# Wave 0's second product by half blocks, an earlier weight queue, and one cast on another engine

## The chip, the cores and the metric

One NeuronCore of a Trainium2 chip. It has a matrix engine (TensorE, "PE" in the profile, with "PEld" for its weight loads), a vector engine (VectorE, "DVE"), a scalar engine (ScalarE, "ACT"), a general one (GpSimd, "POOL"), and a queue engine that issues most transfers (SyncE, "SP"). Each runs its own list of instructions in order and waits on semaphores for the others. The metric is the device time of one execution, in microseconds; less is better.

## The reference

Lightning attention over blocks of 64, its result laid out as tokens by features, then a feed-forward layer with a sigmoid gate:

```python
for b in range(nb):                     # blocks of 64 along the sequence, kv_state carried on
    intra = np.einsum('bhic,bhjc->bhij', qb, kb) * Dmask[None]
    intra = np.einsum('bhij,bhjd->bhid', intra, vb)
    inter = np.einsum('bhid,bhde->bhie', qb * lam_pow[None], kv_state)
    out[:, :, sl] = intra + inter
    kv_state = lam_block * kv_state + np.einsum('bhsd,bhse->bhde', kb * rev_pow[None], vb)
...
x = attn_out.transpose(0, 2, 1, 3).reshape(B * S, H * D)      # 3072 tokens x 512
h = x @ w_in                                                  # w_in 512 x 2048
g = h * (1.0 / (1.0 + np.exp(-1.702 * h)))
return g @ w_out                                              # w_out 2048 x 512
```

q, k and v are 4 batches x 8 heads x 768 x 64, float32.

## The kernel before

The 3072 tokens are worked in six waves of 512. Waves 0 and 1 (`ND = 2`) take two batches one after the other (`c` = 0 and 1, 256 tokens of each); waves 2 to 5 take 128 tokens of all four batches. A wave loads k, q and v; casts k and q to bf16 with the decay factors (`do_cast`); transposes them (`turn_pe` on TensorE in waves 0 and 1, `turn_dma` by transfer later); forms masked scores, state and output (`start` and `end` in waves 0 and 1); writes the attention result, transposed, to `xT`; then runs the feed-forward layer.

**First product** (`x @ w_in`, to 16 slices `fc` of `g_sb`). Wave 0 does it plainly: `mlp1_half` for slices 0 to 3 by batch, `mlp1` for 4 to 15. Wave 1 does half of its slices plainly (`mlp1_half`, the four pairs in `HALVES`, for both batches), and the rest, like waves 2 to 5, by a scheme of seven half-block products instead of eight (`in_product`, steps `a1`, `a7v`, ... in `STEPS`). That scheme needs sums of weight blocks (`in_sums(g)`, four VectorE operations or eight smaller ones for each of four groups `g`) and of `xT` blocks (`x_sums`, four operations).

**Second product** (`g @ w_out`). Wave 0 does it plainly in `mlp2(w, g, j)`: for each group `g` of 128 tokens and chunk `j` of w_out, four matmuls of 128x512, 64 in all; a VectorE copy of each finished group, and its two stores later. Waves 1 to 5 use the seven-product scheme: `product(w, n, ts)` runs product `n` for token tile `t` as eight matmuls of 128x256 into one of three accumulator banks (Q for n = 2; V for 7 and 4; X for 1, 6, 5, 3). Products 2, 4, 5, 3 complete an output block, and 1, 7, 6 leave a part that ScalarE copies out before the next product adds to the same bank (`after_product`). It needs sums of `g_sb` (`g_sums`, steps `gl..` for the low half of the slices, `gh..` for the high half; s1 to s4 of the step's digits) and of w_out chunks (`weight_sums(j)`, four operations for each of four chunks).

**Order.** Inside `manual_schedule` the order of the program is the order on each engine. `side` holds (position, function) pairs for attention and sums, `main` the matrix work of waves 0 and 1; a side item comes ahead of the main item of its number. Waves 2 to 5, and wave 1 from step `a1` on, follow the strings in `STEPS` by `one_step`. So the attention of wave 1 is threaded between the `mlp2` items of wave 0 (positions 19 to 34), `in_sums` stand at 5, 6, 7 and 10, `weight_sums(0..2)` at 14, and `weight_sums(3)` at 2.5 of wave 1's slices.

**Queues.** GpSimd issues the weight transfers, which convert to bf16 (w_in in five chunks of 2, 3, 4, 4 and 3 slices, w_out in four), and batch 1's v of wave 0, in between its own casts. SyncE issues k, q and v, the stores, and the DMA transposes, in program order. Wave 1's loads are kept behind a tiny transfer that reads w_out chunk 1 (`gate_sync`, line 710), so that they start when that chunk has landed. k and q have one buffer per batch slot, so a load waits for the cast of the data before it.

Of the kernel before, what the change touches and what calls it, by code (L numbers as in the profile page):

```python
# [25 lines left out]
def kernel(  # L26
# [13 lines left out]
    nc = tc.nc  # L40
# [3 lines left out]
    P = 128  # L44
# [398 lines left out]

    CHAIN = {1: "X", 6: "X", 5: "X", 3: "X", 2: "Q", 7: "V", 4: "V"}

    def product(w, n, ts):
        last = w == NW - 1
        key = ts[0] if last else 0
        if n == 1 and (last or ts[0] == 0):
            for c in "QVX":  # L450
                blocks[w, c, key] = acc(f"ps_{c}", shape=[P, 2, 256], tag="a" if last and ts[0] else "mm")
        bank = blocks[w, CHAIN[n], key]
        sums, raw = half_sum.get(w, [None] * 4), [[token_half(w, i, kh) for kh in range(2)] for i in range(2)]
        x = {1: raw[0][0], 2: raw[0][1], 4: raw[1][1], 5: sums[0], 6: sums[1], 7: sums[2], 3: sums[3]}[n]
        for t in ts:
            for m in range(FFC // 2):
                y = {1: (0, 0), 2: (1, 0), 3: (1, 1)}.get(n)
                y = w_half(m, *y) if y else TS[{4: 3, 5: 0, 6: 1, 7: 2}[n]][:, m]
                nc.tensor.matmul(bank[:, t], x[:, m, t * P : (t + 1) * P], y,  # L459
                                 start=(n in (1, 2, 7) and t == ts[0] * last and m == 0),  # L460
                                 stop=(m == FFC // 2 - 1), skip_group_check=True)
        if last or ts[-1] == 1:
            t = slice(ts[0], ts[0] + 1) if last else slice(0, 2)
            if n == 2 and 0 < w < NW - 1:
                c11[w] = partial(after_product, w, n, bank, t)
            else:
                after_product(w, n, bank, t)
# [27 lines left out]
    GR = {w: (1, 2, 0, 3) if w > 1 else (0, 3) for w in range(1, NW)}  # L495
    TAGS = {w: ("aQXV", "mXVQ", "aQXV", "aXVQ") if w > 1 else ("aQXV", "aXVQ") for w in range(1, NW)}
    HALVES = (0, 2, 5, 7)
    IN_SUMS_AT, X_AT, T_AT = ((5, 1), (6, 2), (7, 3), (10, 0)), 3.5, 2.5
    GROUPS = (((4, 13), (14, 15)), ((0, 2), (1, 3)), ((6, 5), (8, 7)), ((10, 9), (12, 11)))
    USED = sorted({g for w in range(NW) for g in GR.get(w, ())})  # L500
    TI = {g: [const.tile([P, KC // 2, 2, P], bf16, name=f"w_in_t{g}{n}") for n in range(1, 5)] for g in USED}
# [59 lines left out]
        a, b = (GROUPS[g][u][j] for u in range(2))  # L561
        nc.scalar.activation(g_of[w][:, a : b + 1 : b - a, 256 * i : 256 * i + 256], bank, GELU)  # L562

    late = []

    def mlp2(w, g, j):
        if j == 0:
            o_ps[w, g] = acc("ps_out", shape=[P, d_model], tag="mm")
        ps_out = o_ps[w, g]
        for fc in range(j * CW, (j + 1) * CW):  # L570
            nc.tensor.matmul(ps_out, g_of[w][:, fc, g * P : (g + 1) * P], w_out_sb[j][:, fc % CW, :],  # L571
                             start=(fc == 0), stop=(fc == FFC - 1))
        if j == NCH - 1:
            o = op.tile([P, d_model], f32, tag="o", name="o_sb")
            nc.vector.tensor_copy(o, ps_out)
            r0 = g // 2 * S + (g % 2) * P

            def store():
                for a, rows in enumerate((A, Z)):
                    nc.sync.dma_start(out=out[r0 : r0 + P].rearrange("(s a) d -> s a d", a=2)[:, a, :], in_=o[rows])  # L580
            late.append(store)

    def mlp_items(w):
        if w < ND:
            items = [(mlp1_half, w, c, fc) for c in range(HF) for fc in ((0, 2), HALVES)[w] if w or c or fc]
            if w == 0:
                items += [(mlp1, w, fc) for fc in range(4, FFC)]
        if w == 0:
            items += [(mlp2, w, g, j) for j in range(NCH) for g in range(3)]
            return items + [(mlp2, w, 3, j) for j in range(NCH)]  # L590
        return items + [(one_step, w, s) for s in STEPS[w].split()]

    def one_step(w, s):
        if s[0] == "+":
            w, s = w + 1, s[1:]
# [1 line left out]
        if s[0] == "f":  # L597
            mlp1(w, int(a))
        elif s[0] in "abcd":
            k = "abcd".index(s[0])  # L600
            in_product(w, GR[w][k], int(s[1]), TAGS[w][k], dve_copy if s[2:] == "v" else act_copy)
        elif s[0] in "ABCD":
            in_gelu(w, GR[w]["ABCD".index(s[0])], int(a))
        elif s[0] == "P":
            product(w, int(s[1]), (int(s[2]),))
        elif s[0] in "kq":
            do_cast(x, int(a), s[0], nc.vector)
        elif s[0] in "KQ":
            do_cast(x, int(a), s[0].lower(), nc.gpsimd)
        elif s[0] == "t":  # L610
            turn_dma(x, int(s[2]), s[1])
        elif s[0] == "v":
            cast_v(x, int(s[1]), ((act_copy, dve_copy)[s[2:] == "v"],))
        elif s[0] == "S":
            n_scores(x, int(a))
        elif s[0] == "M":
            n_masks(x, int(a))
        elif s[0] == "m":
            n_masks(x, int(a), True)
        elif s[0] == "R":  # L620
            n_rest(x)
        elif s[0] == "o":
            c11.pop(w)()
        elif s[0] == "X":
            x_sums(x)
        elif s[0] == "G":
            gate_pool(x_sum[w][3][0:1, 0, 0:1])
        elif s[0] == "g":
            m0, m1 = {"l": (0, 4), "h": (4, 8)}[s[1]]
            g_sums(w, m0, m1, tuple(int(c) - 1 for c in s[2:]))  # L630
        elif s[0] == "L":
            load(w + (1 if a == "w" else 2), "kq" if a == "k" else "v")
        else:
            raise ValueError(s)

    STEPS = {
# [24 lines left out]
    with tc.manual_schedule():  # L661
# [18 lines left out]
        d_scores(0, 0, 0)  # L680
        d_scores(0, 0, 1)
        fill(3)
        for g in range(2):
            do_cast(0, 1, "k", nc.gpsimd, g)
        for j in (1, 2):
            load_w_in(j)
        d_one(0, 0, "mm")
        d_keep(0, 0)
        turn_pe(0, 1, "k", act_copy, 0)
# [2 lines left out]
        d_state(0, 0, states[0, 0], Z)  # L692
        do_cast(0, 1, "q", nc.vector, 0)
        do_cast(0, 1, "q", nc.vector, 1)
        turn_pe(0, 1, "k", dve_copy, 1)
        d_x(0, 0, 0, oa, act_copy)
        turn_pe(0, 1, "q", act_copy, 0)
        d_inter(0, 0, oz, 0, False)
        turn_pe(0, 1, "q", dve_copy, 1)
        d_x(0, 0, 1, oz, act_copy)  # L700
        fill(1, "a")
        d_scores(0, 1, 0, True)
        cast_v(0, 1, (act_copy, pool_copy))
        for j in range(3, len(IN_CH)):
            load_w_in(j)
        for j in range(NCH):
            load_w_out(j)
        nc.gpsimd.affine_select(mask, mask, pattern=[[0, 1], [1, P]], channel_multiplier=-1, base=0,
                                compare_op=mybir.AluOpType.is_ge, fill=0.0)
        gate_sync(w_out_sb[1][0:1, 0, 0:2])  # L710
# [31 lines left out]
            if w and c == 0:  # L742
                d_keep(w, 1)

        def stores():
            for f in late:
                f()

        side, main = [(0, (end, 0, 1))], []
        for w in range(ND):  # L750
            n = len(main)
            main += mlp_items(w)
            e = len(main)
            x = w + 1
            if x < ND:
                for c, (k_at, q_at, v_at, k_turn, q_turn, s_at, e_at) in enumerate(
                        ((19, 20, 19, 24, 25.5, 27, 30), (26.5, 28, 28, 29, 30, 32, 34))):
                    side += [(n + k_at, (do_cast, x, c, "k", (nc.vector, nc.gpsimd)[c])),
                             (n + q_at, (do_cast, x, c, "q", nc.vector)),
                             (n + v_at, (cast_v, x, c, ((pool_copy, pool_copy), (act_copy, act_copy))[c])),  # L760
                             (n + k_turn, (turn_pe, x, c, "k", act_copy)),
                             (n + q_turn, (turn_pe, x, c, "q", act_copy)),
                             (n + s_at, (start, x, c)), (n + e_at, (end, x, c))]
            else:
                for c in range(HF):
                    for t, nm in ((n + (2.1, 4.1)[c], "k"), (n + (3, 5)[c], "q")):
                        side += [(t, (do_cast, x, c, nm, nc.gpsimd)), (t, (turn_dma, x, c, nm))]
                side += [(n + 1, (stores,)), (n + 7, (load, x, "v")), (n + X_AT, (x_sums, w)), (n + T_AT, (weight_sums, NCH - 1))]
            if w == 0:
                side += [(n + t, (in_sums, g)) for t, g in IN_SUMS_AT]  # L770
                side += [(n + 14, (weight_sums, j)) for j in range(NCH - 1)]
                side += [(n + 12, (load, w + 2, "kq"))]
        side.sort(key=lambda x: x[0])
        for i, (f, *a) in enumerate(main):
            while side and side[0][0] <= i:
                _, (g, *b) = side.pop(0)
                g(*b)
            f(*a)
        for _, (g, *b) in side:
            g(*b)  # L780
        for w in range(ND, NW):
            for s in STEPS[w].split():
                one_step(w, s)


# [28 lines left out]
```

## Time and profile before

| | |
|---|---|
| times of three runs | 193.36, 193.69, 196.18 us; median 193.69 |
| the profiled execution | 194.36 us, of it 192.7 us of span |
| granted TensorE clock | 1.00 in every stretch that was read |
| wave 1's first slice (line 414) | starts 49.89, the first complete in sequence at 50.05 |
| step a1 of wave 1 (line 543) | starts 58.83 |
| first scores of wave 2 (line 335) | start 67.27 |
| HBM | 27.26 MB read, 6.29 MB written |

The page gives busy time by engine, the span in 40 slices, the transfer queues, the chain of work that ended last, and the costliest groups of instructions. Other views of the same execution list the instructions in order of time, that chain in order of time, and busy time by stretch. Start times are counted from the start of the span. In the order of time, "x4" is the number of merged instructions, and the brackets at the end tell how long the engine had been idle and what ended that. Matmuls overlap, so a group's shown length is longer than the time until the next one can start.

### The profile page before, as it was taken

The page shows a single profiled execution, that of the slowest core. Times are in us where ns is not written, and L with a number is a line of the kernel's source. Part 1 is how long each engine was busy: PE and PEld are TensorE (multiplying, and loading weights), DVE is VectorE, ACT ScalarE, POOL GpSimd, SP SyncE. Part 2 cuts the span into 40 slices and gives each one's busy share as a digit, 9 for nine tenths or more (in the row PEclk, how much of TensorE's full clock was granted, in tenths as well). Part 3 has the DMA queues.
Part 4 walks back from the last instruction along what each step waited for, and adds up shares of the span by engine and source line. Part 5 has one row for each costly group of instructions (what it writes and reads, how often), then busy time and mean ns, then how long its engine had stood idle before and what let it go on. Part 6 is the DMA issues. An engine that isn't in the chain of part 4 may idle for free.

```text
span 192.7 us, 5432 instructions
## 1 busy us (share of the span) xinstructions
PE 184.8 (96%) x2243; PEld 146.3 (76%) x2249; DVE 152.2 (79%) x288; ACT 127.4 (66%) x238; POOL 50.9 (26%) x73
## 2 busy tenths in 40 slices
PE   7779999999999999999999999999999999999993
PEld 2357644446788888888888888888888888888882
DVE  1886775189799899878799979799879797889950
ACT  4867764035776886479896388896388885597711
POOL 5478200034593000097000195000393000000000
PEclk9999999999999999999999999999999999999999
DMA  5999999999989699874989846999366903300113
GB/s 160 315 239 196 198 200 207 262 274 282 242 222 194 127 258 240 212 180 113 209 202 223 247 113 156 210 231 250 136 141 139 218 0 110 113 0 3 48 58 111
DMA packets 89087, 33.90 MB, mean 176 GB/s; under 512 B 67431, under 2 KB 88423, under 8 KB 89063
## 3 DMA queue, kind: packets, MB, share of 16 engines
q1 hardware_dynamic: 84164, 28.84, 60.7%
q0 software_dynamic: 4896, 4.72, 14.5%
q8 instruction: 17, 0.28, 0.6%
q14 instruction: 8, 0.06, 0.1%
q10 hardware_dynamic: 2, 0.00, 0.0%
HBM read 27.26 MB, written 6.29 MB: 174 GB/s over the span
## 4 chain that ended last, share of the span: by engine, by line
PE 76%; DMA 16%; DVE 2%; POOL 2%; SPq 1%; issue 0%; ACT 0%; ACTq 0%
PE ps_X L459 18%; PE ps_hX L543 16%; PE ps_V L459 9%; PE ps_hV L543 8%; DMA w_out<-in_moe_w_out_dram 6%; PE ps_Q L459 5%; PE ps_hQ L543 4%; DMA kf<-in_k_dram 4%; DMA vf<-in_v_dram 3%; PE ps_out L571 3%; PE ps_h L414 3%; DMA qf<-in_q_dram 3%; PE ps_s L335 2%; PE ps_o L390 2%; POOL w_in L181 1%; PE ps_o L377 1%
## 5 line engine op out<-in xcount | busy, mean ns | idle before, releaser
L459 PEld LDWEIGHTS <-g_s 128*128 128x128 bf16 x320 | 30.9, 98 | 4.1
L562 ACT ACTIVATE g_sb<-h_sb 128x512 bf16<-128x512 f32 x54 | 32.6, 631 | 1.2 <-DVE h_sb L551 1.2
L543 PEld LDWEIGHTS <-w_in_t 128*128 128x128 bf16 x288 | 28.1, 98 | 3.8 <-issue 0.5
L221 ACT COPY part<-ps_hX 128x512 f32<-128x512 f32 x32 | 18.3, 586 | 11.9 <-PE ps_hX L543 11.9
L459 PEld LDWEIGHTS <-g_sb 128*128 128x128 bf16 x240 | 22.8, 98 | 3.4
L543 PEld LDWEIGHTS <-w_in 128*128 128x128 bf16 x216 | 21.1, 98 | 2.4
L543 PE MATMUL ps_hX<-x_s,w_in_t 128*128 128x256 bf16 x144 | 21.6, 272 | 0.0
L459 PE MATMUL ps_X<-w_out_t,g_s 128*128 128x256 bf16 x160 | 19.1, 273 | 0.0
L439 DVE TENSOR_TENSOR g_s<-g_sb 128x1024 bf16<-128x1024 bf16 x20 | 13.7, 687 | 5.8 <-ACT g_sb L562 5.6
L209 POOL TENSOR_TENSOR ks<-kf,k_pow 128x512 bf16<-128x512 f32 x16 | 16.6, 1062 | 3.1 <-PE ps_kv L279 3.1
L209 POOL TENSOR_TENSOR qs<-qf,q_pow 128x512 bf16<-128x512 f32 x16 | 16.6, 1062 | 2.0 <-PE ps_h L414 2.0
L656 POOL CAST behind_q<-x_s 1x1 f32<-1x1 bf16 x3 | 0.5, 175 | 62.3 <-DVE x_s L528 62.3
L218 DVE COPY part<-ps_hV 128x512 f32<-128x512 f32 x18 | 12.4, 688 | 3.2 <-PE ps_hV L543 3.2
L571 PE MATMUL ps_out<-w_out,g_sb 128*128 128x512 bf16 x60 | 14.3, 379 | 0.2
L551 DVE TENSOR_TENSOR h_sb<-part,ps_hX 128x512 f32<-128x512 f32 x18 | 12.3, 681 | 2.7 <-PE ps_hX L543 2.7
L551 DVE TENSOR_TENSOR h_sb<-part,ps_hV 128x512 f32<-128x512 f32 x18 | 12.3, 684 | 1.0 <-PE ps_hV L543 1.0
L221 ACT CAST v_sb<-vf 128x1024 bf16<-128x1024 f32 (+1 forms) x13 | 11.3, 884 | 2.2 <-DMA vf<-in_v_dram 2.2
L551 DVE TENSOR_TENSOR h_sb<-part,ps_hQ 128x512 f32<-128x512 f32 x18 | 12.2, 680 | 0.0
L562 ACT ACTIVATE g_sb<-ps_hX 128x512 bf16<-128x512 f32 x18 | 10.6, 588 | 1.8 <-PE ps_hX L543 1.8
L472 ACT COPY part<-ps_X 128x512 f32<-128x512 f32 (+1 forms) x12 | 6.1, 511 | 8.1 <-PE ps_X L459 8.1
L414 PE MATMUL ps_h<-xT,w_in 128*128 128x256 bf16 x96 | 11.3, 273 | 0.0
L348 DVE SCALAR_TENSOR_TENSOR sm<-ps_s,inv_pow,mask 128x512 bf16<-128x512 f32 x16 | 11.2, 744 | 0.0
(112 smaller groups left out, 362.4 us busy)
## 6 DMA issues: line engine op xcount, KB each, us to landing
kf<-in_k_dram SPq DMA_DIRECT2D x10, 512.0 KB, 7.0
qf<-in_q_dram SPq DMA_DIRECT2D x10, 512.0 KB, 6.6
vf<-in_v_dram SPq DMA_DIRECT2D x10, 512.0 KB, 6.1
out_dram<-o_sb SPq DMA_DIRECT2D x24, 128.0 KB, 2.4
out_dram<-o_sb SPq DMA_DIRECT2D x12, 256.0 KB, 2.1
w_out<-in_moe_w_out_dram POOLq DMA_DIRECT2D x4, 512.0 KB, 13.3
kf<-in_k_dram SPq DMA_DIRECT2D x4, 256.0 KB, 3.1
qf<-in_q_dram SPq DMA_DIRECT2D x4, 256.0 KB, 4.9
```

Source lines behind the costliest of these rows:

```text
L209: eng.tensor_tensor(x.rearrange("p b (r i j d) -> p j (b r) i d", i=2, j=2, d=D)[:, j], f.rearrange("p h (a d) -> p (h a) d", a=2).rearran ...
L218: nc.vector.tensor_copy(out, in_)
L221: nc.scalar.copy(out, in_)
L348: nc.vector.scalar_tensor_tensor(sm, s, inv_pow[:, n : n + 1], mask.to_broadcast([P, B, P]), op0=MUL, op1=MUL)
L414: nc.tensor.matmul(h[:, u, :], w_in_sb[j][:, kc, i * P : (i + 1) * P], xT[w][:, kc, cols], start=(kc == 0), stop=(kc == KC - 1))
L439: nc.vector.tensor_tensor(o, x, y, op=f)
L459: nc.tensor.matmul(bank[:, t], x[:, m, t * P : (t + 1) * P], y, start=(n in (1, 2, 7) and t == ts[0] * last and m == 0), stop=(m == FFC // ...
L472: nc.scalar.copy(part[w, n, t.start][:, t], bank[:, t])
L543: nc.tensor.matmul(bank[:, u], z[:, kc], y[:, kc], start=(n in (1, 2, 7) and u + kc == 0), stop=(kc == 1), skip_group_check=True)
L551: nc.vector.tensor_tensor(h, h_part[w, g, {2: 1, 5: 7, 4: 6}[n]], bank, op=ADD)
L562: nc.scalar.activation(g_of[w][:, a : b + 1 : b - a, 256 * i : 256 * i + 256], bank, GELU)
L571: nc.tensor.matmul(ps_out, g_of[w][:, fc, g * P : (g + 1) * P], w_out_sb[j][:, fc % CW, :], start=(fc == 0), stop=(fc == FFC - 1))
```

## The change

Wave 0 no longer has `mlp2`. Its second product is run by `product`, which gains an argument `ms`, the slice pairs to take: steps `p1a`, `p2a`, `p1b`, `p2b`, `p7l`, `p1h`, `p2h`, `p7h` run products 1, 2 and 7 in pieces by chunks of w_out, then `p4l`, `p4h`, and `P60` to `P31` as in other waves. `g_sums` for wave 0 and `weight_sums(3)` stand in wave 0. The positions of `side` and `main` give way to an order written out. `in_sums(2)` (step `I2`) moves to wave 1, behind `gh3`. Among GpSimd's instructions, w_in chunk 1 goes between the two halves of a k cast, and all other weight chunks directly behind it; half of wave 0's v cast of batch 1 goes from GpSimd to VectorE; wave 1's q cast of batch 1 goes from VectorE to GpSimd. Wave 0's stores are issued as its blocks are completed.

```diff
-    def product(w, n, ts):
+    def product(w, n, ts, ms=range(FFC // 2)):
...
-        if n == 1 and (last or ts[0] == 0):
+        if n == 1 and (last or ts[0] == 0) and ms[0] == 0:
...
-            for m in range(FFC // 2):
+            for m in ms:
...
-        if last or ts[-1] == 1:
+        if (last or ts[-1] == 1) and ms[-1] == FFC // 2 - 1:
             t = slice(ts[0], ts[0] + 1) if last else slice(0, 2)
-            if n == 2 and 0 < w < NW - 1:
+            if n == 2 and w < NW - 1:
...
+        elif s[0] == "p":
+            product(w, int(s[1]), (0, 1), {"a": range(4), "b": range(4, 6), "l": range(6), "h": range(6, 8)}[s[2]])
+        elif s[0] == "W":
+            weight_sums(int(a))
+        elif s[0] == "I":
+            in_sums(int(a))
...
-        1: ("a1 a7v a2 a6 b1 b7v A2 a5 b2 b6 B2 a4 a3 b5 b4 A5 P10 A4 b3 gl3 B4 B5 P11 gh3 S0 S1 M0 P20 m1 "
+        1: ("a1 a7v a2 a6 b1 b7v A2 a5 b2 b6 B2 a4 a3 b5 b4 A5 P10 A4 b3 gl3 B4 B5 P11 gh3 I2 S0 S1 M0 P20 m1 "
...
-        for g in range(2):
-            do_cast(0, 1, "k", nc.gpsimd, g)
-        for j in (1, 2):
+        do_cast(0, 1, "k", nc.gpsimd, 0)
+        load_w_in(1)
+        do_cast(0, 1, "k", nc.gpsimd, 1)
+        for j in range(2, len(IN_CH)):
             load_w_in(j)
+        for j in range(NCH):
+            load_w_out(j)
...
-        turn_pe(0, 1, "k", dve_copy, 1)
         d_x(0, 0, 0, oa, act_copy)
         turn_pe(0, 1, "q", act_copy, 0)
         d_inter(0, 0, oz, 0, False)
+        turn_pe(0, 1, "k", dve_copy, 1)
...
-        cast_v(0, 1, (act_copy, pool_copy))
-        for j in range(3, len(IN_CH)):
-            load_w_in(j)
-        for j in range(NCH):
-            load_w_out(j)
+        cast_v(0, 1, (act_copy, dve_copy))
...
+        end(0, 1)
+        for c, fc in ((0, 2), (1, 0), (1, 2)):
+            mlp1_half(0, c, fc)
+        for fc in range(4, FFC):
+            mlp1(0, fc)
+            steps(0, {5: "I1", 7: "I3", 9: "I0 gl3 gl1", 11: "W0 gl2", 13: "W1 gl4"}.get(fc, ""))
+        steps(0, "p1a gh3 p2a W2 p1b p2b p7l W3 p1h p2h p7h")
+        do_cast(1, 0, "k", nc.vector)
+        steps(0, "p4l")
+        do_cast(1, 0, "q", nc.vector)
+        turn_pe(1, 0, "k", act_copy)
+        steps(0, "p4h gh1 gh2 o")
+        load(2, "kq")
+        cast_v(1, 0)
+        do_cast(1, 1, "k", nc.gpsimd)
+        turn_pe(1, 0, "q", act_copy)
+        steps(0, "P60")
+        start(1, 0)
+        steps(0, "P61 gh4")
+        cast_v(1, 1, (act_copy, act_copy))
+        do_cast(1, 1, "q", nc.gpsimd)
+        turn_pe(1, 1, "k", act_copy)
+        steps(0, "P50 P51")
+        end(1, 0)
+        turn_pe(1, 1, "q", act_copy)
+        steps(0, "P30 P31")
+        halves = [(c, fc) for c in range(HF) for fc in HALVES]
+        for i, (c, fc) in enumerate(halves):
+            if i == 1:
+                start(1, 1)
+            if i == 3:
+                end(1, 1)
+            if i == 4:
+                x_sums(1)
+            mlp1_half(1, c, fc)
+            if i in (1, 2, 3, 4):
+                nm = "kq"[(i - 1) % 2]
+                do_cast(2, (i - 1) // 2, nm, nc.gpsimd)
+                turn_dma(2, (i - 1) // 2, nm)
+            if i == 6:
+                load(2, "v")
+        steps(1, STEPS[1])
```

`steps(w, names)` runs `one_step` for each name in turn.

More of the change, by code (lines that the diff above doesn't have):

```diff
@@ L497 @@
     HALVES = (0, 2, 5, 7)
-    IN_SUMS_AT, X_AT, T_AT = ((5, 1), (6, 2), (7, 3), (10, 0)), 3.5, 2.5
     GROUPS = (((4, 13), (14, 15)), ((0, 2), (1, 3)), ((6, 5), (8, 7)), ((10, 9), (12, 11)))
@@ L562, in in_gelu @@
         nc.scalar.activation(g_of[w][:, a : b + 1 : b - a, 256 * i : 256 * i + 256], bank, GELU)
[L564 to L591, printed above, removed]
     def one_step(w, s):
@@ L743, in end @@
                 d_keep(w, 1)
[L745 to L780, printed above, removed]
+        def steps(w, names):
+            for s in names.split():
+                one_step(w, s)
+        end(0, 1)
[4 more added lines that the diff above has]
+            steps(0, {5: "I1", 7: "I3", 9: "I0 gl3 gl1", 11: "W0 gl2", 13: "W1 gl4"}.get(fc, ""))
@@ L781 @@
+        steps(1, STEPS[1])
         for w in range(ND, NW):
-            for s in STEPS[w].split():
-                one_step(w, s)
+            steps(w, STEPS[w])
 _INS = ['q', 'k', 'v', 'lam', 'moe_w_in', 'moe_w_out']
```

## The prediction

> **What bounds the kernel now.** I read the page's busy line first, then the chain of work that ended last between 7 and 62 us, then the order of time around each edit, then the DMA windows. The busy line:
>
> ```profile
> PE 184.8 (96%) x2243; PEld 146.3 (76%) x2249; DVE 152.2 (79%) x288; ACT 127.4 (66%) x238; POOL 50.9 (26%) x73
> ```
>
> TensorE is nearly always busy, so a matmul saved is time saved only where nothing else ends last. From 18 to 62 us something else does. The chain there (start, length, what):
>
> ```profile
> 17.97 12.37 DMA w_out<-in_moe_w_out_dram
> ...
> 31.23 7.09 DMA kf<-in_k_dram
> ...
> 38.35 1.44 DVE ks L202 x4
> 39.79 0.05 issue
> 39.83 0.40 PE ps_t L238 x4
> 40.23 1.73 PE ps_out L571 x8
> ...
> 57.26 1.25 DVE w_out_t L426
> 58.52 0.33 DVE kv L739
> 58.85 0.87 DVE x_s L528
> 59.71 0.04 issue
> 59.76 0.60 PE ps_hV L543 x4
> ```
>
> The weights land, only then does SyncE's gate let wave 1's k load go, it lands at 38.35, is cast and transposed. TensorE lived off `mlp2` meanwhile. At the end the last `weight_sums` hold up `x_sums`, and TensorE (its a1 issued 58.83 to 59.27) waits until 59.76: 0.49 us.
>
> Why that `weight_sums` was slow (order of time; start, length, engine):
>
> ```profile
> 34.04 0.42 DVE L426 TENSOR_TENSOR w_out_t<-w_out,w_out_t 128x512 bf16<-128x512 bf16 x1
> ...
> 53.72 1.24 DVE L426 TENSOR_TENSOR w_out_t<-w_out 128x512 bf16<-128x512 bf16 x1
> ...
> 54.63 2.42 POOL L209 TENSOR_TENSOR ks<-kf,k_pow 128x512 bf16<-128x512 f32 x2
> ```
>
> Alone such an operation takes 0.42 us; beside GpSimd's casts 1.24, as long as one cast (1.21). The two engines seem to take turns, one instruction each.
>
> **The product itself.** Out: 64 matmuls 128x512, 1.73/8 = 0.216 each, 13.84 us. In: 7 x 16 matmuls 128x256 at 0.87/8 = 0.109, 12.2 us. TensorE work falls by 1.6. VectorE gains eight `g_sums` (0.69 each, 0.65 apart) and three adds (0.68) and loses four copies (0.69): +4.5; ScalarE gains four copies of 0.59, uncovered once (below).
>
> **Weight queue.** In the built order w_in1 now goes out between the two halves of the k cast: w_in0's issue 7.74 + 0.95, v 8.68 + 0.92, two casts of 0.58 from 9.74, so about 10.9 instead of 12.01. What that can win, by DMA windows (DMA share is the second last column but one):
>
> ```profile
> 13.00:14.00 1.00, 0.47 (x9) 0.25 (x7) 0.92 (x3) 0.83 (x2) 0.57 (x1) 1.00 0.76 246
> 14.00:15.00 1.00, 1.00 (x34) 0.67 (x36) 0.70 (x3) 0.31 (x2) 0.00 (x0) 1.00 0.91 141
> 15.00:16.00 1.00, 1.00 (x24) 0.76 (x14) 1.00 (x2) 1.00 (x3) 0.78 (x2) 1.00 1.27 187
> ```
>
> Against the 1.23 of 18 to 33 us, 0.47 + 0.32 = 0.79 is missing, 0.65 us of transfer. Later the stream is full, so no more than this comes from issuing earlier. I take 0.6, bounds 0 and 0.65. Gate, k landing (37.75), v landing (41.41 before, 40.8 after) move by it.
>
> **v cast of batch 1 to VectorE.** GpSimd's 0.61 goes; VectorE's is between 0.42 (bf16 copy) and 0.69 (f32 from PSUM), in front of the last two masks, so wave 0's second half starts up to 0.5 late (I take 0.3). The wait for k at 38 hides it. The k transposes moved behind `d_inter` wait for casts that end at 12.8 instead of 12.06, ahead of the q copy that releases the scores: 0.
>
> **Wave 0's product, step by step** (first matmul near 31.5). X, Q and V take the accumulators of slices 13, 14 and 15, free in time. p1a, p2a, p1b, p2b (24 matmuls) to 34.15; p7l to 35.5, its sums done by 33.9; w_out3 lands near 35.0 (issued about 19.4, 16.2 to landing, less 0.6); p1h, p2h, p7h to 36.8. p4l adds to V's bank, so it waits for ScalarE's copy of p7: 0.2 + 0.58 + 0.05, to 37.6; ends 38.9. Before, 36 wide matmuls ended at 39.1, so this wait is covered by that for k.
> k cast 37.75 to 39.2, q cast to 40.65 (1.43 each); k transposes end 39.5, p4h 39.95, q transposes 40.9. Then P60 needs s2: gh1, gh2 stand on VectorE behind both casts, and GpSimd's two v casts (0.58 each) start at 40.8 beside them. Alone gh2 ends at 41.95; taking turns, gh1 to 41.3, v cast to 41.9, gh2 to 42.55, v cast to 43.1. P60's first four matmuls end at 41.35, so TensorE stands 1.2 us, ends P60 at 43.05, and `start(1,0)` begins at 43.2, when the v casts are done: exactly where it begins in the trace (43.20). But there 16 wide matmuls were left (3.46), now 40 narrow ones (4.37): +0.9. P50 adds to the bank that ScalarE copies after P61: 0.3 of its 0.59 lie behind the k transposes, 0.3 don't, less 0.15 of issue gaps. In all wave 1's first slice (50.05 before) starts near 51.1: **+1.05**, between -0.1 (below, rival one) and +1.65.
>
> The Trainium skill, "SBUF — State Buffer", "Who interferes with whom", states that a VectorE instruction with two SBUF inputs and a GpSimd one that reads SBUF exclude each other, whole instruction by whole instruction. By it gh2 ends at 42.55; by a third of the speed under overlap, which the 1.24 allows as well, at 43.3, and the sum is 0.65 higher (rival two). The trace's 1.24 beside 1.21 agrees with the Trainium skill.
>
> **What leaves wave 1's start.** The last `weight_sums` is now done near 36.4, so `x_sums`, in front of slice five, are ready well before a7: **-0.49**. Batch 1's q cast on GpSimd (2.32 instead of 1.43) follows its k cast, 45.5 to 47.8, its transposes come at 48.9: covered by 1.1.
>
> **in_sums(2) in wave 1.** It ran in VectorE's idle time at 20.76; now it stands behind gh3, in front of M0. VectorE there:
>
> ```profile
> 67.65 0.69 DVE L439 TENSOR_TENSOR g_s<-g_sb 128x1024 bf16<-128x1024 bf16 x1 [0.72 <-ACT g_sb L562]
> 68.26 1.41 DVE L348 SCALAR_TENSOR_TENSOR sm<-ps_s,inv_pow,mask 128x512 bf16<-128x512 f32 x2
> ...
> 77.52 1.66 DVE L368 SCALAR_TENSOR_TENSOR kv<-kv,blk_pow,ps_kv 128x256 bf16<-128x256 bf16 x4 [0.15 <-PE ps_kv L364]
> 79.62 0.69 DVE L483 TENSOR_TENSOR o_sb<-part,ps_X 128x512 f32<-128x512 f32 x1 [0.44 <-PE ps_X L459]
> ```
>
> Four sums cost 1.45. From 68.26 to 79.62 VectorE idles 0.15 + 0.44. P30 (80.37) adds to the X bank that this last add reads (to 80.31), so 1.45 - 0.59 = 0.86 comes through, less a 0.06 gap: **+0.8**, bounds 0 and 1.45. Who waits behind: M0, all g_s, kv, that add.
>
> **Other moves.** Wave 0's stores leave the start of wave 1 for wave 0; two of them now stand on SyncE ahead of wave 2's loads and wait for VectorE's add (43.2). See rival three. Wave 2's casts on GpSimd stand behind the new q casts too, but these end at 47.8 and the loads land later than that; 45.0 + 7.0 to landing + 8.9 of casts is 61, seven before the scores: 0.
>
> **Sum.** 1.05 - 0.49 + 0.8 = +1.36. The profiled execution takes 194.36 us (span 192.7 and 1.66 around it), so 195.7 under the profile; the median shown is 193.69, so **195.0**.
>
> **Rivals.**
> One, no slower: VectorE keeps ahead. Place: P60's fifth matmul. It decides if gh2 ends before 41.35, and `in_sums(2)` falls into idle time. For it: VectorE is busy 79% only. Against: both casts stand in front and can't start before k lands. TensorE then waits only for the v casts (42.0), then for batch 1's k casts; the first slice starts within 0.1 of 50.05. With -0.49: 193.2; with the transfers and P50's copy at their best, 192.7.
> Two: under overlap VectorE runs at a third instead of taking turns: +0.65, and if the weight queue gains nothing another 0.6: 195.7 to 196.3. For it the 1.24 alone; against it, its match with 1.21.
> Three: wave 2's loads come too late. Their first issue was 41.34; two stores of 0.9 (8 took 7.16) behind 43.2 put it at 45.0, 3.7 later. The last transpose ended at 64.66, its scores begin at 67.27: 2.6 of room plus 0.56 that TensorE is later. If all 3.7 comes through, 0.5 to 2 more: 195.6 to 197.1. Against: GpSimd waited 3.1 and 2.05 us for TensorE before those casts, which the lateness uses up first.
> Four: the queue edit does nothing (w_in1's descriptors no sooner at the engines): 195.6.
>
> **Numbers.** Forecast (194.2 to 195.6, with four) 0.47, one 0.25, two 0.14, three 0.10, unknown 0.04. Range 192.6 to 197.1, from one's best to three's end. A measurement of this kernel can tell about 2% (3.9 us) from no change. Faster than that would need more than the 1.6, 0.49 and 0.6 together: 0.04 for the unknown. Slower needs three on top of two, or the unknown: 0.10. Within: 0.86.
>
> **What would show it.** Right: w_out3's sums about 0.6 earlier; the k cast near 37.75; an idle TensorE of 1 us or more in front of P60's fifth matmul with gh2 ending last; gh1 or gh2 longer than 0.69; no wait at a7; P30 of wave 1 late by 0.8 behind VectorE's add. Wrong: P60 running through, a k landing earlier than 37, GpSimd's casts ending after 62, or scores of wave 2 waiting for a transpose.

## The result, and the profile after

The kernel after takes 194.8 us at the median of 20 runs (193.83 to 197.13), the kernel before 193.32 (192.57 to 196.18, 20 runs): a ratio of 1.0076, 95% interval [1.0051, 1.0100]. That is 1.5 us more, well resolved, and no change by the 2% that the forecast used. The forecast was 195.0. The profiled execution after took 195.65 us, 193.9 of it span, against 194.36 and 192.7 before: the two spans differ by 1.2. In both, and in every profile below, the granted TensorE clock was 1.0 between 5 and 160 us wherever it was read.

The busy line of the page, after:

```profile
PE 185.0 (95%) x2295; PEld 151.6 (78%) x2297; DVE 154.1 (79%) x292; ACT 129.9 (67%) x242; POOL 54.1 (28%) x76
```

The chain of work that ended last, after, between 7 and 64 us (start, length, what):

```profile
17.62 18.74 DMA w_out<-in_moe_w_out_dram
...
36.85 1.09 DVE w_out_t L426 x3
37.94 1.34 DVE ks L202 x4
39.28 1.34 DVE qs L202 x4
...
41.26 0.99 DVE g_s L439
...
42.30 0.61 PE ps_X L459 x4
...
59.94 0.44 PE ps_hX L542 x4
60.37 0.44 PE ps_hV L542 x4
```

Before, this chain went from chunk 1 of w_out over SyncE's gate to the landing of k. Now it goes from the last chunk of w_out straight through VectorE: weight sums, k cast, q cast, two sums of g, and only then TensorE. Between a1 (59.94 in the chain) and a7 (60.37), where `x_sums` stood before, nothing is left.

The same stretch in order of time, after (idle time ahead and what ended it in brackets), with wave 1's first slice and step P30 behind it:

```profile
36.40 0.60 PE L459 MATMUL ps_X<-w_out,g_sb 128*128 128x256 bf16 x4 [0.80 <-DMA w_out<-in_moe_w_out_dram]
...
38.93 1.47 PE L459 MATMUL ps_V<-w_out_t,g_sb 128*128 128x256 bf16 x12 [0.67 <-ACT part L472]
...
40.70 2.02 POOL L215 CAST v_sb<-vf 128x512 bf16<-128x512 f32 x2 [21.97 <-DMA vf<-in_v_dram]
...
41.26 0.98 DVE L439 TENSOR_TENSOR g_s<-g_s,g_sb 128x1024 bf16<-128x1024 bf16 x1
...
45.70 1.91 PE L459 MATMUL ps_X<-w_out_t,g_s 128*128 128x256 bf16 x16 [0.23 <-ACT part L472]
...
50.83 1.04 PE L414 MATMUL ps_h<-xT,w_in 128*128 128x256 bf16 x8
...
81.53 1.69 PE L459 MATMUL ps_X<-w_out,g_s 128*128 128x256 bf16 x14 [0.25 <-DVE o_sb L483]
```

TensorE stands 0.80 for the last chunk, 0.67 for ScalarE's copy of V, and 0.22 in between for the chunk's sums. The row at 45.70 is P50, which waits for ScalarE's copy of product 6. The last row is P30, which waits for VectorE's add, 11 us behind the four sums of `in_sums(2)` (68.73 to 70.28). In the kernel before, the first matmuls behind the same transposes of k, and P30, stand here:

```profile
46.52 1.03 PE L571 MATMUL ps_out<-w_out,g_sb 128*128 128x512 bf16 x4
...
80.37 1.91 PE L459 MATMUL ps_X<-w_out,g_s 128*128 128x256 bf16 x16
```

Step by step against the trace of before: wave 1's first slice starts at 50.83 instead of 49.89 (+0.94), step a7 at 60.21 instead of 59.76 (the lead has shrunk to 0.45, so 0.49 came back), P30 at 81.53 instead of 80.37 (+1.16, so 0.71 more). 0.94 - 0.49 + 0.71 = 1.16, the difference of the spans.

Where TensorE's saving went, by the windows (length; busy time of PE, PEld, DVE, ACT, POOL; clock; DMA share; GB/s), after:

```profile
33.00:45.00 12.00, 10.15 (x139) 8.20 (x138) 8.92 (x21) 3.90 (x7) 4.30 (x7) 1.00 1.02 288
```

and for the kernel before:

```profile
33.00:45.00 12.00, 11.62 (x111) 5.82 (x112) 7.27 (x17) 2.83 (x5) 3.11 (x6) 1.00 0.99 274
```

The dip of the transfers at 13 to 15 us is filled (a DMA share of 1.01 and 1.27, where it was 0.76 and 0.91). But of the 12 us from 33 to 45 TensorE stands for 1.85 where it stood for 0.38: 1.47 of idle time has come in, nearly the 1.6 us of matmul work that the product saves.

### The profile page after: what moved, and what is told of

Read it like the earlier page. It is cut to its first block, busy times and chain, and to the rows that moved or that the text cites. A ratio compares the mean times of both kernels' runs of the same rounds, so it can differ in the third digit from the quotient of the medians.

```text
span 193.9 us, 5541 instructions
## 1 busy us (share of the span) xinstructions
PE 185.0 (95%) x2295; PEld 151.6 (78%) x2297; DVE 154.1 (79%) x292; ACT 129.9 (67%) x242; POOL 54.1 (28%) x76
## 4 chain that ended last, share of the span: by engine, by line
PE 69%; DMA 12%; DVE 9%; POOL 5%; ACT 1%; issue 1%; SPq 1%; ACTq 0%
PE ps_X L459 19%; PE ps_hX L542 16%; DMA w_out<-in_moe_w_out_dram 10%; PE ps_hV L542 8%; PE ps_V L459 7%; PE ps_hQ L542 4%; PE ps_Q L459 4%; PE ps_h L414 4%; DVE g_s L439 3%; DMA qf<-in_q_dram 3%; POOL w_in L181 2%; PE ps_s L335 2%; PE ps_o L390 2%; POOL ks L202 1%; DVE sm L348 1%; POOL w_out L185 1%
## 5 line engine op out<-in xcount | busy, mean ns | idle before, releaser
L459 PEld LDWEIGHTS <-g_s 128*128 128x128 bf16 x384 | 36.8, 98 | 6.7 <-issue 1.2
L459 PEld LDWEIGHTS <-g_sb 128*128 128x128 bf16 x288 | 27.5, 98 | 5.9 <-issue 1.8
L459 PE MATMUL ps_X<-w_out_t,g_s 128*128 128x256 bf16 x192 | 23.5, 273 | 0.5 <-ACT part L472 0.2
L439 DVE TENSOR_TENSOR g_s<-g_sb 128x1024 bf16<-128x1024 bf16 x24 | 16.3, 688 | 5.8 <-ACT g_sb L561 5.6
L472 ACT COPY part<-ps_X 128x512 f32<-128x512 f32 (+1 forms) x14 | 7.3, 522 | 13.9 <-PE ps_X L459 13.9
L459 PE MATMUL ps_X<-w_out,g_sb 128*128 128x256 bf16 x96 | 12.6, 273 | 0.8 <-DMA w_out<-in_moe_w_out_dram 0.8
L459 PE MATMUL ps_Q<-w_out,g_sb 128*128 128x256 bf16 x96 | 12.5, 273 | 0.0
L459 PE MATMUL ps_V<-w_out_t,g_sb 128*128 128x256 bf16 x96 | 11.8, 273 | 0.7 <-ACT part L472 0.7
L267 DVE TENSOR_TENSOR sm<-ps_s,mask_d 128x512 bf16<-128x512 f32 x14 | 8.8, 684 | 3.8 <-PE ps_s L259 3.6
L459 PE MATMUL ps_V<-w_out_t,g_s 128*128 128x256 bf16 x96 | 11.6, 273 | 0.2 <-DVE w_out_t L426 0.2
```

Of the source, the lines that this page charges most:

```text
L267: nc.vector.tensor_tensor(sm.rearrange("p i a s -> p i (a s)"), flat, mask_d.rearrange("p o a b s -> p o (a b s)").to_broadcast([P, 2, 2 * ...
L439: nc.vector.tensor_tensor(o, x, y, op=f)
L472: nc.scalar.copy(part[w, n, t.start][:, t], bank[:, t])
```

## The experiments

Times are medians in us; the kernel before had a median of 193.45 beside e1 to e4, 193.51 beside e5 to e8, 193.29 beside e9 to e12. Ratios are to it.

| | what | median | ratio, 95% |
|---|---|---|---|
| | after | 194.80 | 1.0076 [1.0051, 1.0100] |
| e1 | after, in_sums(2) back in wave 0 | 194.08 | 1.0026 [0.9999, 1.0052] |
| e2 | after, gh1 gh2 ahead of W3 | 194.39 | 1.0048 [1.0019, 1.0076] |
| e3 | after, startup of before | 195.07 | 1.0088 [1.0055, 1.0120] |
| e4 | after, gate on chunk 2 of w_out | 195.57 | 1.0106 [1.0057, 1.0154] |
| e5 | e1 and e2 together | 193.74 | 1.0004 [0.9975, 1.0032] |
| e6 | before, startup of after | 193.59 | 1.0013 [0.9977, 1.0048] |
| e7 | before, last weight_sums in wave 0 | 193.34 | 0.9987 [0.9956, 1.0018] |
| e8 | e6 and e7 together | 194.41 | 1.0048 [1.0020, 1.0076] |
| e9 | e5, P60 ahead of p4l | 193.62 | 1.0016 [0.9995, 1.0038] |
| e10 | e9, startup of before | 194.00 | 1.0044 [1.0027, 1.0061] |
| e11 | before, a second profile | 193.30 | 1.0001 [0.9986, 1.0015] |
| e12 | after, a second profile | 194.92 | 1.0076 [1.0050, 1.0102] |

**e1, the sums of w_in group 2 back in wave 0.**

```diff
-  1: ("a1 a7v ... P11 gh3 I2 S0 S1 M0 ..."
+  1: ("a1 a7v ... P11 gh3 S0 S1 M0 ..."
...
-  steps(0, {5: "I1", 7: "I3", ...}.get(fc, ""))
+  steps(0, {5: "I1", 6: "I2", 7: "I3", ...}.get(fc, ""))
```

> The changed kernel with in_sums(2) back in wave 0, behind in_sums(1), where VectorE waits for w_in chunk 3 (2.03 us idle at 22.83 in the changed kernel's trace). My theory: in wave 1 the four sums (68.73 to 70.20) go, P60's wait for gh2 (0.18) and P30's wait for VectorE's add go, so P30, now 81.53 and 0.71 later than the shift at a7 (0.45) explains, comes at 80.8 to 80.9 and the time falls by 0.7 us, to about 1.0040 of the kernel before. Rival: TensorE would have stood there for another reason (scores, ScalarE copies), and P30 stays at 81.3 or later, time unchanged within 0.2 us.

The median falls by 0.72. From a7 (59.35) to P30 it takes 20.62, as before (20.61) and not 21.32 as after, and P30 has no wait in front of it. P30 in order of time, e1:

```profile
79.97 1.91 PE L459 MATMUL ps_X<-w_out,g_s 128*128 128x256 bf16 x16
```

So the moved sums cost 0.70 us, all of it in front of P30.

**e2, the two sums that P60 needs, ahead of the last weight sums.**

```diff
-  steps(0, "p1a gh3 p2a W2 p1b p2b p7l W3 p1h p2h p7h")
+  steps(0, "p1a gh3 p2a W2 p1b p2b p7l gh1 gh2 W3 p1h p2h p7h")
...
-  steps(0, "p4h gh1 gh2 o")
+  steps(0, "p4h o")
```

> The changed kernel with gh1 and gh2 ahead of the last weight_sums, where VectorE is idle 2.29 us until 36.39. My theory: gh1 and gh2 take 0.65 each in that gap, TensorE's 0.41 us of idle before P60's fifth matmul goes, the two v casts on GpSimd run beside no VectorE work and end near 41.9 instead of 42.72, start(1,0) comes at 42.3 to 42.4 instead of 42.84, wave 1's first slice at 50.5 instead of 50.99, and the time falls by 0.4 to 0.5 us. Rival: the casts of k and q and not gh2 end last, and start(1,0) stays at 42.7 or later.

The median falls by 0.41. In order of time, e2:

```profile
40.13 1.17 POOL L215 CAST v_sb<-vf 128x512 bf16<-128x512 f32 x2 [21.46 <-DMA vf<-in_v_dram]
...
40.52 1.04 PE L459 MATMUL ps_X<-w_out_t,g_s 128*128 128x256 bf16 x8
```

P60 runs through, eight in one row. GpSimd's two v casts take 1.17 here; in after, with the sums of g beside them, 2.02. The first slice starts 12.43 us behind the k cast where it was 12.97. The order of the two sums is a real cost, 0.4 to 0.5.

**e3, the startup of before, and e4, a later gate.**

```diff
 e3:
-  do_cast(0, 1, "k", nc.gpsimd, 0); load_w_in(1); do_cast(0, 1, "k", nc.gpsimd, 1)
-  for j in range(2, len(IN_CH)): load_w_in(j)
-  for j in range(NCH): load_w_out(j)
+  do_cast(0, 1, "k", nc.gpsimd, 0); do_cast(0, 1, "k", nc.gpsimd, 1)
+  for j in (1, 2): load_w_in(j)
...
-  cast_v(0, 1, (act_copy, dve_copy))
+  cast_v(0, 1, (act_copy, pool_copy))
+  for j in range(3, len(IN_CH)): load_w_in(j)
+  for j in range(NCH): load_w_out(j)
 e4:
-  gate_sync(w_out_sb[1][0:1, 0, 0:2])
+  gate_sync(w_out_sb[2][0:1, 0, 0:2])
```

> The changed kernel with GpSimd's order of before: both k casts first, then w_in 1 and 2, then its half of the v cast, then the other weights. My theory: the DMA share at 13 to 15 us falls back from 1.01 and 1.27 to about 0.76 and 0.91, w_in chunk 3 lands 0.5 us later (22.83 to 23.3), the gate opens at 30.36 instead of 29.84, k cast starts 0.5 later, and with it the first slice of wave 1: the time rises by 0.4 to 0.6 us. Rival: the last w_out chunk sets the k cast (VectorE was at its sums until 37.86), and since that chunk landed 0.7 us later in the changed kernel than in the one before although it was issued earlier, its landing does not move, and the time stays within 0.2 us.

> The changed kernel with the gate of wave 1's loads on w_out chunk 2 instead of 1, about 2.4 us later. My theory: the last w_out chunk landed late (36.36, I had forecast 35.0) because wave 1's k, q and v share the transfer engines with its tail; with the later gate it lands at 34.9 to 35.3, TensorE's 0.80 us wait for it goes, but k lands at 38.3 or later, so start(1,0) moves by -0.2 to +0.8 us. Rival: the tail of the chunk is slow by itself (36.2 or later whatever the loads do), and only the later k shows: start(1,0) later by 0.5 us or more.

e3 is 0.27 slower than after by the medians; the intervals overlap widely, so the startup edit is worth 0.3 or nothing. Its k cast starts at 36.85, between the two of after (37.86, and 36.55 in e12 below), so the half microsecond of the theory doesn't show there. In e4 the sums of the last chunk start at 34.27, sooner than theory or rival had it. That doesn't show that wave 1's loads had held the chunk: it landed 5.1 us behind chunk 1 in e4, and 5.2 behind it in e1 and e12, where the gate is on chunk 1. Only the profile after has 6.5, and why stays open. In order of time, e4:

```profile
39.16 1.43 DVE L202 TENSOR_TENSOR qs<-qf,qd_pow 128x256 bf16<-128x256 f32 x4 [0.92 <-DMA qf<-in_q_dram]
```

TensorE no longer waits for the chunk, and the kernel is no faster: VectorE waits 0.98 for k, whose cast starts at 36.81, and 0.92 for q. `start(1,0)` comes at 42.81, as in the profile after (42.84). TensorE's 0.80 for the chunk is therefore not a price by itself. What counts is when VectorE gets through both casts, and the late chunk's sums hold them up in the one profile, the landing of q in the other.

**e5, e1 and e2 together.**

> The kernel after with both undone at once: in_sums(2) back in wave 0 behind I1, and gh1 gh2 ahead of the last weight_sums. Theory (the two prices are separate waits at separate places: 0.70 of P30 behind VectorE's add, about 0.5 of P60's fifth matmul behind gh2): the gains add up, 194.8 - 0.7 - 0.45 = 193.6, ratio to before 1.000 to 1.002; first slice of wave 1 near 49.5, from a7 to P30 20.6. Rival (the first slice is bound by the landing of k, so that gh early only changes which wait shows): no better than with in_sums(2) alone, 194.1, ratio 1.003.

The two gains add up, and the ratio is 1.0004: with both undone the kernel is as fast as before, within 0.3%. The first slice is at 49.58, from a7 to P30 20.63. The theory of two separate prices holds. What is left of the change, the half-block product with the moved weight sums, casts and startup, brings together neither a gain nor a loss that this interval (0.6 us to each side) can tell. The half-block product was not run without the rest.

**e6 to e8, the other parts put on the kernel before.** e6 takes the startup lines (e3's diff backwards, with the k transposes behind `d_inter`), e7 this, and e8 both:

```diff
-  side += [..., (n + X_AT, (x_sums, w)), (n + T_AT, (weight_sums, NCH - 1))]
+  side += [..., (n + X_AT, (x_sums, w))]
...
-  side += [(n + 14, (weight_sums, j)) for j in range(NCH - 1)]
+  side += [(n + 14, (weight_sums, j)) for j in range(NCH)]
```

> The kernel before with the startup part alone: weights issued ahead of the second cast, w_out ahead of the masks, batch 1's v cast on VectorE, k transposes behind d_inter. Theory of the prediction: w_out3 lands 0.6 earlier, the gate opens 0.6 earlier, k lands 0.6 earlier and everything behind its wait moves with it: ratio 0.997. Rival (the stream to w_out3 is limited elsewhere, or k's landing is limited by what lands behind the gate): ratio 0.999 to 1.001.

> The kernel before with the last weight_sums moved into wave 0, beside the other three. Theory: the wait at a7 (0.49) goes, and nothing else is late: ratio 0.9975, a7 at 59.3 in a profile like that of before. Rival (VectorE waits for w_out3 in front of the copies of wave 0's product and the k cast, so that 0.42 of it or more comes back there): ratio 0.999 to 1.002.

> The kernel before with the startup part and the moved weight_sums, without the half-block product. Theory: both add up, 0.6 + 0.49: ratio 0.9945, 192.4. Rival (the queue part is worth nothing): ratio 0.9975 as with the moved weight_sums alone. A second rival (both worth nothing): 1.000.

e6 went by the rival: no gain that its interval can tell. In its profile the chain of work that ended last says why, between 17 and 50 us:

```profile
21.61 10.09 PE ps_h L402 x46
...
32.40 7.07 PE ps_out L571 x32
39.47 0.45 PE ps_t L238 x8
```

No transfer and no cast is in it any more. TensorE has run from its first wide matmul at 21.18 on without a stop of more than 0.05: the transfers came early enough, so TensorE's own work ends last, and that started 0.3 to 0.9 later than in the two profiles of before (20.87 and 20.33). e7's interval holds both its theory and its rival and decides nothing. In its profile, VectorE starts on the last chunk at 36.24 and the k cast follows at 37.71 without a wait for k, so the moved sums, in front of that cast, can hold it. e8 is by the medians slower than either part alone (its interval overlaps that of e6), which neither theory nor rival allowed. Its profiled execution (193.72 us) was faster than its median and shows one delay that the others lack: batch 1's q cast on VectorE takes 2.30 instead of 1.42, beside casts of GpSimd, and from the first slice to a1 it takes 0.16 more than in e6. Why the two together cost 0.9 stays open.

**e9 and e10, P60 in the idle time in front of p4l**, on top of e5; e10 with e3's startup as well.

```diff
-  steps(0, "p4l")
+  steps(0, "P60 p4l")
...
-  steps(0, "p4h o")
+  steps(0, "o")
...
-  steps(0, "P60")
+  steps(0, "p4h")
```

> As with in_sums(2) back and gh1 gh2 early, and in addition product 6's first half put ahead of p4l, with p4h in its old place. Theory (behind the cast of k the TensorE still has 40 narrow matmuls where before had 16 wide ones, so the first slice is the landing of k plus that work; each matmul that runs in a gap ahead of it is time gained): P60 runs while ScalarE copies V, the 0.67 of idle TensorE in front of p4l goes, start(1,0) at or before 41.2 where it was 41.6, first slice 49.1, median 193.3, ratio 0.998. Rival (the copies of the k and q transposes on ScalarE set start(1,0), not the TensorE's work): scores no earlier than 41.9, first slice 49.5, ratio 1.000 as without it.

> The same with the startup of before (weights after both casts, batch 1's v cast on GpSimd). Theory (the queue edit brings w_out3 0.3 to 0.6 earlier, and TensorE's start of the first product 0.3 to 0.6 later by the cast on VectorE; behind the half-block product it is the stream of weights that decides, so the queue edit must help here): slower than with the startup of after by 0.2 to 0.5, ratio 1.000. Rival (the edit is worth nothing, or its v cast costs as much): equal, ratio 0.998.

In order of time, e9:

```profile
37.66 1.47 PE L459 MATMUL ps_V<-w_out_t,g_sb 128*128 128x256 bf16 x12
...
41.60 0.64 PE L259 MATMUL ps_s<-qT,kT 64*64 64x128 bf16 x32 [0.76 <-ACT qT L221]
```

The wait in front of p4l is gone, `start(1,0)` begins at 40.40, and its scores then wait 0.76 for ScalarE's copy of the transposed q. The first slice starts at 49.13, 12.75 behind the k cast (36.38); in e5 it was 12.67. So the theory's 49.1 came, but by an early k cast; the saving itself was taken by the ScalarE copies, as the rival said, and the median is e5's within 0.12, the ratio 1.0016 and not 0.998. e10 is 0.38 slower than e9, with intervals that overlap a little: here the startup edit helps by 0.2 to 0.5 as expected, though not beyond doubt. Neither kernel beats before. Putting P61 ahead as well, to fill that 0.76, was not tried.

**e11 and e12, second profiles of before and after.**

> The kernel before, unchanged, for a second profile of it: which of its waits belong to every execution. Theory (k's landing swings from execution to execution, and the first slice of wave 1 is 11.5 behind the k cast or 28.4 behind the first wide matmul of wave 0, whichever is later): k cast between 36.8 and 38.4, first slice between 49.0 and 49.9 and on that rule, the wait at a7 between 0 and 0.5. Rival (the profile shown is typical): k cast at 38.3, wait at a7 0.49. Ratio 1.000 within 0.3%.

> The kernel after, unchanged, for a second profile of it. Theory (the first slice is 13.0 behind the k cast whatever the landing of the last chunk of w_out): w_out3 anywhere between 34.8 and 36.4, k cast between 36.8 and 37.9, first slice 13.0 after it, no wait at a7, P30 21.3 behind a7. Rival (the late w_out3 of 36.36 is part of the change): w_out3 at 36.4 and TensorE idle 0.8 again. Ratio 1.0076 within its interval.

In order of time, before once more (span 191.1):

```profile
36.93 1.43 DVE L202 TENSOR_TENSOR ks<-kf,kd_pow 128x256 bf16<-128x256 f32 x4 [2.71 <-DMA kf<-in_k_dram]
...
48.72 1.04 PE L414 MATMUL ps_h<-xT,w_in 128*128 128x256 bf16 x8
...
57.67 0.60 PE L543 MATMUL ps_hX<-xT,w_in 128*128 128x256 bf16 x4
58.20 0.60 PE L543 MATMUL ps_hV<-x_s,w_in_t 128*128 128x256 bf16 x4
```

and after once more (span 192.7):

```profile
35.08 0.42 DVE L426 TENSOR_TENSOR w_out_t<-w_out 128x512 bf16<-128x512 bf16 x1 [0.93 <-DMA w_out<-in_moe_w_out_dram]
...
36.55 1.42 DVE L202 TENSOR_TENSOR ks<-kf,kd_pow 128x256 bf16<-128x256 f32 x4
...
41.09 0.61 PE L459 MATMUL ps_X<-w_out_t,g_s 128*128 128x256 bf16 x4 [0.23 <-DVE g_s L439]
...
49.62 1.04 PE L414 MATMUL ps_h<-xT,w_in 128*128 128x256 bf16 x8
```

The first profile of before was not typical: k is cast 1.42 earlier here, TensorE never stands for it, and the wait at a7 is 58.20 - 57.67 - 0.44 = 0.09, not 0.49. After's late chunk of w_out was not typical either; TensorE does not stand for it here. The sum of this pair: first slice +0.90, a7 -0.09, from a7 to P30 +0.71 (21.32 against 20.61), together +1.5, and the spans differ by 1.6.

The profiles with the order of before, and those with the order of after, give one rule each. A is the start of TensorE's first wide (128x512) matmul of wave 0, B that of the k cast of wave 1:

| | A | B | first slice | behind A | behind B |
|---|---|---|---|---|---|
| before | 20.87 | 38.35 | 49.89 | 29.02 | 11.54 |
| e11, before again | 20.33 | 36.93 | 48.72 | 28.39 | 11.79 |
| e6 | 21.18 | 37.51 | 49.58 | 28.40 | 12.07 |
| e7 | 20.07 | 37.71 | 49.24 | 29.17 | 11.53 |
| e8 | 21.18 | 36.90 | 49.57 | 28.39 | 12.67 |
| after | 21.15 | 37.86 | 50.83 | 29.68 | 12.97 |
| e12, after again | 20.96 | 36.55 | 49.62 | 28.66 | 13.07 |
| e1 | 21.25 | 36.93 | 49.97 | 28.72 | 13.04 |
| e3 | 20.55 | 36.85 | 49.97 | 29.42 | 13.12 |
| e4 | 20.68 | 36.81 | 50.80 | 30.12 | 13.99 |

With the plain product the first slice is the later of A + 28.39 and B + 11.53, to 0.02 us in all five; both constants were read from these profiles, and e11, which ran last of them, keeps to the rule, though its 48.72 is below the stretch that its expectation named. (e12's k cast, too, came 0.25 before the stretch named for it.) With the half-block product in after's order it is B + 13.0 to 13.1 whatever A is (e4 has 0.9 more, its wait for q). The way behind B has grown by 1.5. The bound behind A is no longer seen, and it has come down with the saved matmuls: e9's first slice is 27.94 behind its A (21.19), less than 28.39.

## Why the prediction was right, and where its terms were not

The sign and the time hold (forecast +1.36, measured 1.5 to 1.6 by the medians and 1.16 and 1.5 by the two pairs of profiles), and so do the two mechanisms that carry the sum: more work behind the wait for k, and sums of VectorE in front of P30. That the sum is so close is in part luck, as errors of the terms offset each other. One by one:

- **First slice, forecast +1.05; measured +0.94 and +0.90.** Two errors offset each other. The forecast left `start(1,0)` where it was, at 43.20; it came 0.36 earlier (42.84), and 0.40 in the second pair (41.63 against 42.03). From there to the first slice it takes 6.69 in both profiles of before and 7.99 in both of after, 1.30 more and not 1.05. The 0.9 of this for the matmuls (40 narrow ones for 16 wide) fits. The wait for ScalarE's copy in front of P50 was put at 0.15 and cost 0.39: from batch 1's transposes of k to the next matmul of the product it takes 0.84 after (44.86 to 45.70) and 0.45 before (46.07 to 46.52). The mechanism was the one named: what is left behind the wait decides, not what is saved in all.
- **P60's wait for gh2, forecast 1.2; measured 0.30 and 0.40.** Its fifth matmul starts 0.41 and 0.51 behind the fourth in the two profiles, where 0.11 is the usual step; the 0.23 in e12's row counts only the time in which no matmul ran. The mechanism (gh1 and gh2 behind both casts) is right and e2 gives its worth, 0.4. The size is off because, counted from the k cast, P60 began 3.71 behind it in both and not 3.2, and gh2 ended 4.4 to 4.5 behind it and not 4.8. P60 was late because TensorE stood 0.67 for ScalarE's copy of V, which the text had "covered by that for k"; it was not covered, as the next point tells.
- **Why k was cast when it was.** Forecast 37.75 as k's landing; k landed at 37.63 and 36.45, and its cast began at 37.86 and 36.55, both times straight behind the weight sums. The forecast had these sums done near 36.4, well ahead of k. The last chunk, forecast at 35.0, landed at 36.36 and 35.06, so chunk and k came together, and the sums ended last.
- **Turns between VectorE and GpSimd (rival two).** gh2 took 0.98 instead of 0.69 and the two v casts 2.02 instead of 1.17. A third of the speed would have made gh2 2.07. Rival two is out. The Trainium skill, "SBUF — State Buffer", "Who interferes with whom", has a VectorE instruction with two SBUF inputs and a GpSimd one that reads SBUF exclude each other. The 0.98, one sum of 0.69 and 0.29 of waiting beside a cast, agrees with the Trainium skill.
- **a7, forecast -0.49; measured -0.49 and -0.09.** Right for the execution that was shown, but most of that wait is missing in the second profile of before, so 0.09 would have been the better term. Moved alone (e7) the sums bring 0.1% with an interval that includes nothing.
- **in_sums(2), forecast +0.8; measured +0.71 in both pairs**, and e1 gives 0.72 by the medians. Place and releaser were as named: P30 behind VectorE's add.
- **Weight queue, forecast 0.6.** k landed 0.70 and 0.45 earlier in the two pairs, its cast came 0.49 and 0.38 earlier, and e3 and e10 give 0.3 and 0.4 by the medians, neither beyond doubt. The last chunk, issued 1.8 and 1.3 earlier, landed 0.73 later in the first pair and 0.13 earlier in the second. TensorE's first wide matmul came 0.28 and 0.63 later, where 0.3 was forecast for the v cast on VectorE and called hidden. It was hidden behind the half-block product, but not in the kernel before, where e6's profile shows TensorE's own work to be the bound. That it is the cast is not shown: in the second pair batch 1's scores, ahead of that cast, already start 0.69 later (14.46 against 13.77).
- **The other rivals.** One is out: VectorE did end last at P60 and P30. Three is out: wave 2's casts end at 61 on GpSimd and its scores start at 67.74, 0.47 behind those of before and less than the first slice is late. Four is not excluded by e3.
- **Batch 1's q cast on GpSimd** was covered, as forecast: TensorE doesn't stand in front of its transposes (48.62 after, 48.57 before).
- **The signs.** As forecast came no wait at a7, a gh2 longer than 0.69 and P30 late behind VectorE's add. Two did not come: the 1 us of idle TensorE in front of P60's fifth matmul, and w_out3's sums 0.6 earlier. One sign of being wrong, k landing before 37, came in the second profile of after (36.45), but in that of before too (36.91), so it tells nothing of the change.

## What to carry to other kernels

Split the time up to a meeting point into the bounds that meet there (here TensorE's work behind A, and the way behind a landing), and count the work of an edit in front of each bound and behind it: matmuls saved ahead of a wait only lengthen the wait, and those added behind it count in full. Small sums moved into a queue that "is idle on average" cost what is left of them after the idle time ahead of the instruction that a matmul waits for (0.7 of 1.45 us for `in_sums(2)`); two such orders cost here 0.7 and 0.4 of the 1.5. And profile the kernel before twice: a wait of half a microsecond may belong to one execution only.

## What the hardware showed beyond the question

The same kernel's transfers land at different times from execution to execution: wave 1's k was there at 38.32 and at 36.91 in the two profiles of before, the last chunk of w_out at 36.36 and at 35.06 in those of after. The spans differed with it, 192.7 and 191.1, 193.9 and 192.7, and this is larger than any single part of the change. In eleven of the fourteen profiles the last chunk lands 5.1 to 5.3 behind chunk 1, whether the gate of wave 1's loads is on chunk 1 or, as in e4, on chunk 2; in the other three it takes 5.7 to 6.5, and no run here shows why.
